# Attention output with tokens on partitions: unscaled probabilities, heads scaled on the way out of the bank, norm in one operation

## The chip, the cores and the metric

The kernel runs on one core of a Trainium2 chip. The metric is the time of one execution on the device, in microseconds (us). Inputs, weights and output are float32 in the chip's memory.

## The reference

2304 tokens of 512 numbers pass through three layers. Only the first, and the norm at the start of the second, are touched by the change.

```python
def _attn_ref(q, k, v):                      # (4, 8, 576, 64) each
    scores = scale * np.matmul(q, k.transpose(0, 1, 3, 2))
    mask = (rel >= 0) & (rel < window)       # window = 64
    scores = np.where(mask, scores, -1000000000.0)
    scores = scores - np.max(scores, axis=-1, keepdims=True)
    attn = np.exp(scores)
    attn = attn / (np.sum(attn, axis=-1, keepdims=True) + 1e-09)
    return np.matmul(attn, v)

def _moe_ref(x, w_gate, w_val, w_out, rms_g):   # x: (2304, 512)
    rms = np.sqrt(np.mean(x * x, axis=-1, keepdims=True) + 1e-06)
    xn = x / rms * rms_g
    g = xn @ w_gate
    silu = g * (1.0 / (1.0 + np.exp(-g)))
    val = xn @ w_val
    return silu * val @ w_out
```

The third layer routes each token to one of eight experts (512 to 1024 to 512, with a ReLU), and scales what comes back.

## The kernel before

The tokens are cut into 18 tiles of 128. `attention_front` loads a tile's queries, keys and values, `attention_tile` computes its attention and its norm, and leaves `xn`, the normed tile with the 512 numbers on partitions (four pieces of 128) as a high and a low half. The second layer, called FFN here, runs over groups of tiles, `GROUPS = [[0, 1], [2], [3], [4], [5]]` with `SIZES = [2, 2, 4, 4, 4, 2]` tiles in each: `ffn_step` multiplies by a block of the gate and value weights (L976 to L978, three matmuls for the products of high and low halves), applies the activation (L988, L993, L1001) and multiplies by the output weights (L1018 to L1020). In the first group `conv` loads the weights and splits them into halves on ScalarE (ACT) and VectorE (DVE), and `save` writes them to memory for the later groups. The attention of later tiles runs between the FFN matmuls of earlier groups. The experts come last.

What a tile does, by line:

- `mmc` (L680, L688) makes the scores. One bank holds four heads: 128 partitions are the 128 queries, four stretches of 128 columns are the four heads' keys. A query looks back 64 tokens, so the upper 64 queries need the 64 keys before the tile and its first 64, the lower 64 the tile's own 128. The host puts the previous tile's last 64 keys in front of each tile's own, so keys come as 192 columns per head pair, 384 KB per tile. Four mask matmuls (L680) and 16 score matmuls (L688) run, each in one 64x64 quarter of TensorE (PE); `c` is the half of the queries and `j` the head of a pair. A float32 matmul shows as two records.
- For each bank: the maximum (L707), its scaling (L711 or L713), four exponentials with their sums (L717), the guard against zero (L724 or L726), the reciprocal (L729), and `nm`, which multiplies the probabilities by it (L462 on DVE or GpSimd, called POOL, or L734 on ACT). Then four transposes (L751) and a copy out of the bank.
- `pv` (L768): 16 matmuls with the values as weights, so that the output has a head pair's 128 numbers on partitions and tokens as columns.
- `sqr` squares that bank into `xf` (L780), `weigh` multiplies it by the norm's weight g into `x` (L462, or L785 on ACT), and `sums` adds the squares over partitions by matmuls with ones (L795): four per tile for tiles 0 to 3, and one for the others, after `add` (L462) has added the four pieces. `mean` (L812, L814) and `root` (L819, on POOL) follow, giving `y`.
- A transpose of `y`, spread over 128 columns (L828), brings the factor onto all partitions, and `norm` multiplies `x` by it (L462). `hi` (L452, L456) and `lo` (L459) make the halves.

The order of the work comes from a planner. `Plan.op` gets for each step its costs on the engines that may do it, the buffers that it reads and writes, and a due time; a table `SHIFT` with a number per due time moves it, and a dictionary `K` holds the planner's other constants. From these the planner makes one fixed order of instructions for each engine and for SyncE (SP), which issues the loads in order. Where its reckoning finds TensorE idle, it places fillers (L624): matmuls on a tile of ones into a bank of their own, read by nobody. `K["warm"]` is the planner's time from which that bank goes to other work.

```python
pl.op(
    {"t": 1.28}, mmc, r=[qt, kt, both_b, masks], w=col, hold=halves, prio=pr + 2 * sg, tiled=True
)
```

Here `t` is TensorE, 1.28 is the planner's reckoned cost, `r` and `w` are what is read and written, and `prio` is the due time.

## Time and profile before

| | us |
|---|---|
| runs | 800.52, 800.59, 801.9 (median 800.59) |
| the profiled execution | 798.19 |
| its span, first to last instruction | 796.5 |
| TensorE busy | 785.2 |
| VectorE busy | 425.5 |
| ScalarE busy | 357.2 |
| GpSimd busy | 63.7 |

Busy times are unions of the recorded instructions of an engine. In the trace a line of TensorE reads: line of the program, operation, output and inputs by their names, the part of the array (64\*64 is a quarter), the moving operand's partitions and columns, the type, and the number of records. An instruction's end is modelled and overlaps the next one's start, so the cost of a group of matmuls is read from its start to the next group's start.

### The profile page before, as it was taken

How to read it: one execution, taken by the hardware profiler on the slowest of the kernel's cores; microseconds unless marked ns; L12 is line 12 of the kernel's file. 1: busy time of each engine (PE TensorE's matmuls, PEld its weight loads, DVE VectorE, ACT ScalarE, POOL GpSimd, SP SyncE). 2: the span in 40 equal slices, each digit the busy share in tenths (PEclk: the TensorE clock that was granted, in tenths of full speed). 3: DMA queues.
4: the chain of work that ended last, by engine and by line, in shares of the span. 5: the costliest groups of instructions: out<-in, count | busy, mean ns of one | idle time of the engine just before them, and what ended most of it. 6: DMA issues, size and time to landing. Idle time of an engine off the chain costs nothing.

```text
span 796.5 us, 14986 instructions
## 1 busy us (share of the span) xinstructions
PE 785.2 (99%) x5760; PEld 678.7 (85%) x5760; DVE 425.5 (53%) x1054; ACT 357.2 (45%) x959; POOL 63.7 (8%) x114
## 2 busy tenths in 40 slices
PE   9999999999999999999999999999999999999995
PEld 8998999988888888888888888899989998999981
DVE  5999998866452335633324322258447646576400
ACT  5988887556141244424341211325345444365311
POOL 2200000012000002000002000020110011020010
PEclk9999999999999999999999999999999999999998
DMA  8888888975541026430024830365195663676320
GB/s 276 310 281 284 296 288 293 292 257 165 182 173 53 28 76 210 153 112 1 1 106 159 306 116 1 110 212 182 60 300 183 202 198 110 214 241 228 139 77 19
DMA packets 51518, 137.30 MB, mean 172 GB/s; under 512 B 6564, under 2 KB 6564, under 8 KB 51444
## 3 DMA queue, kind: packets, MB, share of 16 engines
q1 hardware_dynamic: 48436, 126.78, 47.4%
q0 software_dynamic: 3008, 9.54, 3.2%
q8 instruction: 46, 0.75, 0.4%
q14 instruction: 28, 0.23, 0.1%
HBM read 112.07 MB, written 24.23 MB: 171 GB/s over the span
## 4 chain that ended last, share of the span: by engine, by line
PE 86%; issue 6%; DMA 5%; ACT 1%; DVE 0%; SPq 0%; POOLq 0%; POOL 0%
PE bank L976 13%; PE bank L977 13%; PE bank L978 13%; PE bank L1018 7%; PE bank L1019 6%; PE bank L1020 6%; DMA out_dram<-osb,meta 5%; PE bank L1522 3%; PE bank L1524 2%; PE bank L1523 2%; PE bank L768 2%; PE bank L751 2%; PE bank L688 2%; PE bank L1680 1%; PE bank L1682 1%
## 5 line engine op out<-in xcount | busy, mean ns | idle before, releaser
L976 PE MATMUL bank<-xn,w 128*128 128x256 f32 (+1 forms) x576 | 198.7, 345 | 0.0
L978 PE MATMUL bank<-xn,w 128*128 128x256 f32 (+1 forms) x576 | 193.8, 337 | 0.0
L977 PE MATMUL bank<-xn,w 128*128 128x256 f32 (+1 forms) x576 | 193.8, 336 | 0.0
L976 PEld LDWEIGHTS bank<-xn,w 128*128 128x128 f32 x576 | 108.8, 189 | 14.4 <-issue 0.6
L978 PEld LDWEIGHTS bank<-xn,w 128*128 128x128 f32 x576 | 108.9, 189 | 11.6
L977 PEld LDWEIGHTS bank<-xn,w 128*128 128x128 f32 x576 | 109.0, 189 | 11.3
L993 DVE SCALAR_TENSOR_TENSOR u<-u,bank 128x256 f32<-128x256 f32 (+1 forms) x72 | 39.6, 552 | 91.0 <-ACT u L988 90.6
L1018 PE MATMUL bank<-wo,h 128*128 128x512 f32 x216 | 87.4, 405 | 0.0
L1019 PE MATMUL bank<-wo,h 128*128 128x512 f32 x216 | 84.5, 391 | 0.0
L1020 PE MATMUL bank<-wo,h 128*128 128x512 f32 x216 | 84.4, 391 | 0.0
L988 ACT ACTIVATE u<-bank 128x256 f32<-128x256 f32 (+1 forms) x72 | 35.2, 489 | 98.1 <-PE bank L978 94.4
L459 DVE TENSOR_TENSOR w<-raw,w 128x512 fp32r<-128x512 f32 x112 | 72.8, 687 | 11.3 <-ACT w L452 10.7
L1001 DVE TENSOR_TENSOR u<-u,bank 128x256 f32<-128x256 f32 (+1 forms) x72 | 39.8, 553 | 70.8 <-PE bank L978 69.9
L452 ACT CAST h<-u 128x512 fp32r<-128x512 f32 (+1 forms) x67 | 34.8, 519 | 94.0 <-DVE u L1001 93.5
L452 ACT CAST w<-raw 128x512 fp32r<-128x512 f32 x90 | 51.3, 622 | 25.1 <-DMA raw<-in_moe_w_dram 13.0
L1522 PE MATMUL bank<-xT,w 128*128 128x240 f32 (+4 forms) x192 | 58.3, 304 | 0.0
L1524 PE MATMUL bank<-xT,w 128*128 128x240 f32 (+4 forms) x192 | 57.8, 301 | 0.0
L1523 PE MATMUL bank<-xT,w 128*128 128x240 f32 (+4 forms) x192 | 57.8, 301 | 0.0
L459 DVE TENSOR_TENSOR h<-u,h 128x256 fp32r<-128x256 f32 (+1 forms) x72 | 40.0, 556 | 23.7 <-ACT h L452 23.3
L717 ACT ACTIVATE s<-bank,m 128x128 f32<-128x128 f32 x144 | 50.8, 382 | 0.4
L1020 PEld LDWEIGHTS bank<-wo,h 128*128 128x128 f32 x216 | 40.6, 188 | 8.9
L1018 PEld LDWEIGHTS bank<-wo,h 128*128 128x128 f32 x216 | 40.7, 188 | 8.2 <-issue 0.9
(242 smaller groups left out, 1342.5 us busy)
## 6 DMA issues: line engine op xcount, KB each, us to landing
w<-whd SPq DMA_DIRECT2D x64, 512.0 KB, 4.3
raw<-in_moe_w_dram SPq DMA_DIRECT2D x64, 512.0 KB, 4.8
whd<-w SPq DMA_DIRECT2D x24, 512.0 KB, 6.1
val<-in_v_dram SPq DMA_DIRECT2D x18, 512.0 KB, 6.1
kt<-in_k_dram SPq DMA_DIRECT2D x18, 384.0 KB, 4.7
raw<-in_moe_w_gate_dram SPq DMA_DIRECT2D x12, 512.0 KB, 5.3
raw<-in_moe_w_out_dram SPq DMA_DIRECT2D x12, 512.0 KB, 5.2
raw<-in_moe_w_val_dram SPq DMA_DIRECT2D x12, 512.0 KB, 5.5
```

What stands on the lines that cost most here:

```text
L452: nc.scalar.copy(o, i)
L459: ve[e].tensor_tensor(out=o, in0=i, in1=h, op=ALU.subtract)
L717: nc.scalar.activation(out=s.t[:, h], in_=score()[:, h], func=AF.Exp, bias=mb.t[:, h:h + 1], scale=scale, accum_out=mb.t[:, 4 + h:5 + h],)
L976: nc.tensor.matmul(o, lhsT=h_, rhs=xn.t[:, 0, kk], start=(kk == 0), stop=False)
L977: nc.tensor.matmul(o, lhsT=h_, rhs=xn.t[:, 1, kk], start=False, stop=False)
L978: nc.tensor.matmul(o, lhsT=l_, rhs=xn.t[:, 0, kk], start=False, stop=(kk == KD - 1))
L1018: nc.tensor.matmul(o, lhsT=h.t[:, 0, c], rhs=wo.t[:, 0, f], start=(n == 0), stop=False)
L1019: nc.tensor.matmul(o, lhsT=h.t[:, 0, c], rhs=wo.t[:, 1, f], start=False, stop=False)
L1020: nc.tensor.matmul(o, lhsT=h.t[:, 1, c], rhs=wo.t[:, 0, f], start=False, stop=(n == NF - 1))
L1522: nc.tensor.matmul(o, lhsT=wh, rhs=x.t[:, 0, kk, 0:N], start=(kk == 0), stop=False)
L1523: nc.tensor.matmul(o, lhsT=wh, rhs=x.t[:, 1, kk, 0:N], start=False, stop=False)
L1524: nc.tensor.matmul(o, lhsT=wl, rhs=x.t[:, 0, kk, 0:N], start=False, stop=(kk == KD - 1))
```

## The change

Parts that are computed otherwise:

- Keys are loaded as 128 columns (256 KB). The scores of the upper 64 queries against the 64 keys before the tile read the previous tile's key buffer, so a tile has 24 score matmuls, 16 of 64 columns and 8 of 128 (L697 of the changed program). There are four key buffers where there were three.
- The probabilities go unscaled to the transposes; `nm` is gone. There is one guard and one reciprocal of eight columns per tile.
- `pv` (L828 of the changed program) has the probabilities as weights and the values as moving operand: the output has tokens on partitions and all eight heads' numbers as 512 columns.
- `xr` multiplies each head by its reciprocal while it copies the bank to `x`. `sqr` squares `x` on ACT and adds up along the row. `mean` and `root` stay; `norm` is one operation on DVE, x times the factor of its token times g. For that g is loaded on every partition (256 KB instead of 2 KB). `weigh`, `add`, `sums`, and the transpose of `y` are gone.
- `turn` (L871 of the changed program) transposes the four pieces of `x` into a bank, and `hi` and `lo` read that bank.
- A branch for scores that are made turned is there, for tiles below `K["st"]`, which is 0.

The planner's constants and its whole table are others. The diff, with the table cut to a line of each:

```diff
-    w_r=4, sl=1.2, n_q=4, n_kt=3, n_s=4, n_m=4, n_p=4, n_x=4, n_y=3, n_xf=1, n_val=3, pf=0.1, cold=6.0, late=1, f0=24.0, pw=110.0, pb=0.6, c1a=0, c1v=0, spe=4, lact=0, warm=86.204, wf=2.122, flead=24.233, nwv=1, port=1.0, t0=46.214, pp=93.267,
-    lead=1.781, clead=9.978, stag=2.552, stage=1.001, slack=-0.037, nt=2, look=-0.056, marg=0.752, dw=1.398, ewl=3.278,
-    ews=8.339, xld=43.407, xtn=7.222, mlead=14.712, vb=0.027, vb2=0.339, tb=-0.042, share=0.003, pls=9, phs=9, sf=0, hfs=1.431, stk=-0.015, rlead=7.936, span=0.317, wl=1.841,
+    w_r=4, sl=1.2, n_q=4, n_kt=4, n_s=4, n_m=4, n_p=4, n_x=4, n_xf=1, n_val=3, pf=0.1, cold=6.0, late=1, f0=24.0, pw=110.0, pb=0.6, c1a=0, c1v=0, st=0, lact=0, warm=40.111, wf=1.857, flead=24.233, nwv=1, port=1.0, t0=46.214, pp=93.267,
+    lead=1.781, clead=9.978, stag=2.552, stage=1.001, slack=0.069, nt=2, look=-0.005, marg=0.006, dw=1.434, ewl=3.278,
+    ews=8.339, xld=43.407, xtn=7.222, mlead=14.712, vb=0.304, vb2=0.465, tb=263.445, share=-0.155, pls=9, phs=9, sf=0, hfs=1.431, stk=-4.54, rlead=7.936, span=0.317, wl=1.841,
...
-    -38.8, -23.1, 59.5, 48.6, 13.7, 47.4, -3.4, -27.9, 3.4, -42.8, -38.2, -38.2, -88, -88.6, -42.9, -17.7, 12.7, -45.4, -59.5, -37.3, -7.7, 14.3, 20.9, -27.3,
...
+    14, 3.2, -22.1, -4.4, 3.7, -63.2, 9.9, -2.1, -52.9, -84.3, -89.9, -29.1, -41.5, -40.9, -31, -77.8, -38.7, -21.5, -22.6, -69.6, -71.3, -42.7, -0.5, -0.2,
...
-    g_sb = fixed("g_sb", [P, KD])
+    g_sb = fixed("g_sb", [P, DM])
...
-        {"s": 0.06}, lambda e: nc.sync.dma_start(out=g_sb.t, in_=rms_g.rearrange("(k p) -> p k", p=P)),
-        w=[g_sb], dma=0.22, prio=8,
+        {"s": 0.06}, lambda e: nc.sync.dma_start(out=g_sb.t, in_=rms_g.rearrange("(o d) -> o d", o=1).to_broadcast([P, DM])),
+        w=[g_sb], dma=0.95, prio=8,
...
-    tag("kt", "a", K["n_kt"], [P, 4, 192])
+    tag("kt", "a", K["n_kt"], [P, 4, P])
...
-    tag("m", "a", K["n_m"], [P, 8])
+    tag("m", "a", K["n_m"], [P, 18])
...
-    tag("y", "a", K["n_y"], [P, 2])
...
+    keys = {}
...
+        keys[t] = kt
...
-        pl.op({"s": 0.1}, load_t(k, kt, t), w=[kt], dma=1.4, prio=pr - K["wl"] + 0.1)
+        pl.op({"s": 0.1}, load_t(k, kt, t), w=[kt], dma=0.95, prio=pr - K["wl"] + 0.1)
...
+        turned_too = t < K["st"]
...
+        mb = Buf("m")
+        before = keys[max(t - 1, 0)]
+        parts = ((0, 0, 64, before, 64), (1, 0, P, kt, 0), (0, 64, 64, kt, 0))
...
             for i in range(4):
-                for c in range(2):
+                for c, o, n, src, at in parts:
                     for j, bk in enumerate(col):
                         nc.tensor.matmul(
-                            bk.t[half(c), i * P:(i + 1) * P], lhsT=qt.t[half(j), i, half(c)],
-                            rhs=kt.t[half(j), i, 64 * c:64 * c + P], start=False, stop=(i == 3),
+                            bk.t[half(c), i * P + o:i * P + o + n], lhsT=qt.t[half(j), i, half(c)],
+                            rhs=src.t[half(j), i, at:at + n], start=False, stop=(i == 3 and (c == 1 or o > 0)),
                         )
...
-            {"t": 1.28}, mmc, r=[qt, kt, both_b, masks], w=col, hold=halves, prio=pr + 2 * sg, tiled=True
+            {"t": 1.28}, mmc, r=[qt, kt, before, both_b, masks], w=col, hold=halves, prio=pr + 2 * sg, tiled=True
...
-            def guard(e, mb=mb):
-                if e == "a":
-                    nc.scalar.activation(out=mb.t[:, 4:8], in_=mb.t[:, 4:8], func=AF.Copy, bias=1e-9)
-                else:
-                    ve[e].tensor_scalar(out=mb.t[:, 4:8], in0=mb.t[:, 4:8], scalar1=1e-9, scalar2=None, op0=ALU.add)
-
-            def rc(e, mb=mb):
-                nc.vector.reciprocal(out=mb.t[:, 4:8], in_=mb.t[:, 4:8])
-
-            def nm(e, s=s, mb=mb):
-                if e == "a":
-                    for h in range(4):
-                        nc.scalar.activation(out=s.t[:, h], in_=s.t[:, h], func=AF.Copy, scale=mb.t[:, 4 + h:5 + h])
-                else:
-                    times(e, s.t, s.t, mb.t[:, 4:8].unsqueeze(2).to_broadcast([P, 4, P]))
-
-            pl.op({"v": 0.61}, mx, r=[sc], w=[mb], prio=ps_)
-            pl.op({"v": 0.08, "a": 0.11}, mxs, r=[mb], w=[mb], prio=ps_)
-            pl.op({"a": 1.48}, ex, r=[sc, mb], w=[s, mb], prio=ps_)
-            pl.op({"v": 0.08, "a": 0.11}, guard, r=[mb], w=[mb], prio=ps_)
-            pl.op({"v": 0.09}, rc, r=[mb], w=[mb], prio=ps_)
-            pl.op({"p": 1.02, "v": 0.61, "a": 1.18}, nm, r=[s, mb], w=[s], prio=ps_, lock="pv")
...
+            pl.op({"v": 0.19, "a": 0.1}, mxs, r=[(mb, hf)], w=[(mb, hf)], prio=ps_, lock="pv")
+            pl.op({"a": 1.48}, ex, r=[sc, (mb, hf)], w=[s, (mb, 2 + hf)], prio=ps_)
...
+        px_ = pr + 5 * sg
...
+        def rc(e):
+            nc.vector.reciprocal(out=mb.t[:, 8:16], in_=mb.t[:, 8:16])
+        pl.op(
+            {"v": 0.19, "a": 0.1}, guard, r=[sm] if turned_too else [(mb, 2), (mb, 3)], w=[(mb, 2), (mb, 3)], prio=px_ - 0.05,
+            lock="pv",
+        )
+        pl.op({"v": 0.19}, rc, r=[(mb, 2), (mb, 3)], w=[(mb, 2), (mb, 3)], prio=px_ - 0.04)
...
         def pv(e, bk=bk):
             for i in range(4):
-                for c in range(2):
-                    for j in range(2):
+                for j in range(2):
+                    for c in range(2):
                         hd = 2 * i + j
                         nc.tensor.matmul(
-                            bk.t[half(j), i * P + 64 * c:i * P + 64 * c + 64], lhsT=al.t[:, c, hd * D:(hd + 1) * D],
-                            rhs=pb_[j].t[:, i, half(c)], start=True, stop=True,
+                            bk.t[half(c), hd * D:(hd + 1) * D], lhsT=pb_[j].t[:, i, half(c)],
+                            rhs=al.t[:, c, hd * D:(hd + 1) * D], start=True, stop=True,
                         )
...
+        def xr(e):
+            r = mb.t[:, 8:16].rearrange("p (j i) -> p i j", j=2).unsqueeze(3).to_broadcast([P, 4, 2, D])
+            times(e, x.t.rearrange("p i (j d) -> p i j d", j=2), bk.t.rearrange("p (i j d) -> p i j d", i=4, j=2), r)
+
...
         def sqr(e):
-            nc.scalar.activation(out=sq.t, in_=pair(), func=AF.Square)
-
-        def weigh(e):
+            nc.scalar.activation(out=sq.t, in_=x.t, func=AF.Square, accum_out=mb.t[:, 16:17])
+
...
+                nc.scalar.activation(out=ms, in_=ms, func=AF.Copy, scale=1.0 / DM, bias=1e-6)
             else:
-                times(e, x.t, pair(), g_sb.t.unsqueeze(2).to_broadcast([P, KD, P]))
-
-        pl.op({"t": 1.1}, pv, r=[al, *pb_], w=[bk], hold=[x, sq], prio=px_, rows=0.5)
...
-        def sums(e, bk=bk):
-            for kk in range(n):
-                nc.tensor.matmul(
-                    bk.t[:, 0:2], lhsT=sq.t[:, kk], rhs=ones.t, start=(kk == 0), stop=(kk == n - 1)
-                )
...
-        n = KD
-        if t >= K["spe"]:
-            n = 1
-            pl.op({"p": 1.25, "v": 0.67}, add, r=[sq], w=[sq], prio=pn_, lock="pv")
-        pl.op({"t": 0.224 * n}, sums, r=[sq, ones], w=[bk], hold=[y], prio=pn_, rows=0.05)
...
+            nc.gpsimd.tensor_tensor(out=mb.t[:, 17:18], in0=mb.t[:, 16:17], in1=mhalf.t, op=ALU.pow)
+
+        def norm(e):
+            nc.vector.scalar_tensor_tensor(
+                out=x.t, in0=x.t, scalar=mb.t[:, 17:18], in1=g_sb.t.rearrange("p (k t) -> p k t", t=P), op0=ALU.mult, op1=ALU.mult
+            )
+
+        pl.op({"t": 1.1}, pv, r=[al, *pb_], w=[bk], hold=[x], prio=px_, rows=0.5)
+        pl.op({"v": 0.66}, xr, r=[bk, (mb, 2), (mb, 3)], w=[x], prio=px_ + 0.05)
+        pl.op({"a": 0.66}, sqr, r=[x], w=[sq, (mb, 4)], prio=px_ + 0.06)
+        pl.op({"a": 0.1, "v": 0.19}, mean, r=[(mb, 4)], w=[(mb, 4)], prio=pn_)
+        pl.op({"p": 0.72}, root, r=[(mb, 4), mhalf], w=[(mb, 5)], prio=pn_, lock="pv")
+        pl.op({"v": 0.65}, norm, r=[x, (mb, 5), g_sb], w=[x], prio=pn_)
...
-            {"t": 0.11}, lambda e: nc.tensor.transpose(bk2.t[:, 0:P], y.t[:, 1:2].to_broadcast([P, P]), ident.t),
-            r=[y, ident], w=[bk2], prio=pn_, rows=0.5,
-        )
-
-        def norm(e):
-            both("v", x.t, x.t, bk2.t[:, 0:P].unsqueeze(1).to_broadcast([P, KD, P]), ALU.mult)
-
-        pl.op({"v": 0.65}, norm, r=[x, bk2], w=[x], prio=pn_)
...
+        def turn(e):
+            for kk in range(KD):
+                nc.tensor.transpose(bk2.t[:, kk * P:(kk + 1) * P], x.t[:, kk], ident.t)
+
+        def pair():
+            return bk2.t.rearrange("p (k t) -> p k t", t=P)
+
+        pl.op({"t": 0.43}, turn, r=[x, ident], w=[bk2], prio=pn_ + 0.02, rows=0.5)
         xn_w[p_].append(pl.op(
-            cost(512, "hs"), lambda e: hi_i(e, xn.t[:, 0, :, js], x.t), r=[x], w=[(xn, (j, 0))], prio=pn_, lock="pv"
+            cost(512, "hp"), lambda e: hi_i(e, xn.t[:, 0, :, js], pair()), r=[bk2], w=[(xn, (j, 0))], prio=pn_ + 0.02
         ))
         xn_w[p_].append(pl.op(
-            cost(512, "ls"), lambda e: lo_i(e, xn.t[:, 1, :, js], x.t, xn.t[:, 0, :, js]),
-            r=[x, (xn, (j, 0))], w=[(xn, (j, 1))], prio=pn_, lock="pv",
+            cost(512, "lp"), lambda e: lo_i(e, xn.t[:, 1, :, js], pair(), xn.t[:, 0, :, js]),
+            r=[bk2, (xn, (j, 0))], w=[(xn, (j, 1))], prio=pn_ + 0.02,
         ))
         attn_ops.append(xn_w[p_][-1])
...
-        if name == "q":
+        if name in ("q", "k"):
             a = turned(a)
-        elif name == "k":
-            a = turned(a)
-            own = a.reshape(a.shape[0], P, HEADS // 2, P)
-            a = np.concatenate([np.roll(own[..., WINDOW:], 1, axis=0), own], axis=3).reshape(a.shape[0], P, -1)
```

The order of the loads at the start (SP). `q`, `kt` and `val` are a tile's queries, keys and values; the shapes are partitions by float32 numbers. Before, and then in the changed program:

```order
L656 DMA q_178<-in_q_dram 128x512
L656 DMA q_202<-in_q_dram 128x512
L656 DMA kt_229<-in_k_dram 128x768
L656 DMA val_266<-in_v_dram 128x1024
L656 DMA kt_285<-in_k_dram 128x768
L656 DMA val_317<-in_v_dram 128x1024
```

```order
L658 DMA kt_179<-in_k_dram 128x512
L658 DMA q_200<-in_q_dram 128x512
L658 DMA val_222<-in_v_dram 128x1024
L658 DMA q_269<-in_q_dram 128x512
L658 DMA kt_311<-in_k_dram 128x512
L658 DMA kt_313<-in_k_dram 128x512
```

The keys of the second tile are the fifth load in both; the first two tiles' queries and keys are smaller, and the first tile's values now stand before the second tile's queries.

TensorE just before the first FFN matmul (L976 before, L1017 in the changed program). `s` are probabilities, `p` their transposes, `xf` the squares, `xn` the normed tile:

```order
L688 MATMUL bank_800<-kt_702,q_612 64x128
L795 MATMUL bank_830<-ones,xf_767 128x2 x4
L751 MATMUL bank_844<-ident,s_581 128x128 x4
L976 MATMUL bank_852<-xn,w_604 128x256
L977 MATMUL bank_852<-xn,w_604 128x256
```

```order
L697 MATMUL bank_764<-kt_667,q_684 64x64
L697 MATMUL bank_765<-kt_667,q_684 64x64
L828 MATMUL bank_805<-val_529,p_713 64x64 x2
L828 MATMUL bank_805<-val_529,p_755 64x64 x2
...
L871 MATMUL bank_831<-ident,x_647 128x128 x4
L1017 MATMUL bank_837<-xn,w_635 128x256
```

Where the sums and a transpose of another tile's probabilities stood, a value product and the turn of a tile's `x` stand. Over the whole program the fillers go from 280 to 198: before the first FFN matmul 200 become 152 (46 and 26 before the first and the second score block become 34 and 22), after it 80 become 46. DVE has 1007 instructions for 1082, ACT 795 for 838, POOL 131 for 137.

## Rows read from the trace of the kernel before

**Rows 1.** The page: busy us of each engine; TensorE's granted clock.

```profile
PE 785.2 (99%) x5760; PEld 678.7 (85%) x5760; DVE 425.5 (53%) x1054; ACT 357.2 (45%) x959; POOL 63.7 (8%) x114
...
PEclk9999999999999999999999999999999999999998
```

**Rows 2.** Waits of TensorE: who, for whom, us in total, times, longest.

```profile
PE warm L624 <- DVE ones_b L535: 1.4, 1, 1.4
PE bank L688 <- DMA kt<-in_k_dram: 0.4, 1, 0.4
```

**Rows 3.** Stages: us; busy of PE, PEld, DVE, ACT, POOL; clock; DMA share; GB/s.

```profile
0.00:33.00 33.00, 31.11 (x545) 28.21 (x546) 22.87 (x63) 24.41 (x96) 8.78 (x39) 1.00 0.83 280
33.00:58.00 25.00, 25.00 (x305) 23.26 (x304) 22.72 (x54) 21.45 (x71) 1.28 (x2) 1.00 0.88 297
58.00:150.00 92.00, 91.98 (x822) 84.01 (x822) 85.93 (x195) 74.32 (x186) 3.88 (x5) 1.00 0.88 294
```

**Rows 4.** Fillers alone, by stage: TensorE busy (records); clock; DMA share; GB/s.

```profile
0.00:33.00 33.00, 14.07 (x200) 1.00 0.83 280
33.00:58.00 25.00, 5.30 (x74) 1.00 0.88 297
58.00:100.00 42.00, 0.84 (x6) 1.00 0.85 291
```

**Rows 5.** TensorE's timeline, start of the program: start, us, instruction, records, [idle before].

```profile
1.40 4.14 PE L624 MATMUL warm<-ones_b 128*128 128x128 bf16 x46 [1.40 <-DVE ones_b L535]
...
9.19 1.10 PE L688 MATMUL bank<-kt,q 64*64 64x128 f32 x32 [0.40 <-DMA kt<-in_k_dram]
```

**Rows 6.** TensorE's timeline, 26 us to the first FFN matmul.

```profile
26.37 1.06 PE L624 MATMUL warm<-ones_b 128*128 128x128 bf16 x16
27.26 0.28 PE L828 MATMUL bank<-ident,y 128*128 128x128 f32 x1
27.46 1.15 PE L768 MATMUL bank<-p,val 128*64 128x64 f32 x32
28.55 0.65 PE L751 MATMUL bank<-ident,s 128*128 128x128 f32 x4
...
29.37 1.04 PE L688 MATMUL bank<-kt,q 64*64 64x128 f32 x32
30.35 1.05 PE L795 MATMUL bank<-ones,xf 128*128 128x2 f32 x8
31.26 0.64 PE L751 MATMUL bank<-ident,s 128*128 128x128 f32 x4
31.65 0.36 PE L976 MATMUL bank<-xn,w 128*128 128x256 f32 x1
```

**Rows 7.** TensorE's timeline in the steady stage, 96 to 104 us.

```profile
96.48 0.60 PE L751 MATMUL bank<-ident,s 128*128 128x128 f32 x4
96.91 0.27 PE L828 MATMUL bank<-ident,y 128*128 128x128 f32 x1
96.94 0.36 PE L976 MATMUL bank<-xn,w 128*128 128x256 f32 x1
97.14 0.28 PE L977 MATMUL bank<-xn,w 128*128 128x256 f32 x1
...
102.66 0.28 PE L795 MATMUL bank<-ones,xf 128*128 128x2 f32 x2
102.80 0.48 PE L1018 MATMUL bank<-wo,h 128*128 128x512 f32 x1
103.12 0.39 PE L1019 MATMUL bank<-wo,h 128*128 128x512 f32 x1
```

**Rows 8.** By line and form: count, busy us, mean ns, idle before.

```profile
L462 DVE TENSOR_TENSOR s<-s,m 128x512 f32<-128x512 f32 x27 | 18.6, 689 | 0.5
...
L462 DVE TENSOR_TENSOR x<-bank,g_sb 128x512 f32<-128x512 f32 x13 | 9.0, 691 | 11.3 <-ACT xf L780 10.4 <-PE bank L768 0.8
...
L795 PE MATMUL bank<-ones,xf 128*128 128x2 f32 x60 | 8.0, 230 | 0.0
```

More of the change, by code (lines that the diff above doesn't have):

```diff
@@ L716, in ex @@
+            def ex(e, s=s, score=score, hf=hf):
                 for h in range(4):
+                    at = 4 * hf + h
                     nc.scalar.activation(
[L718 to L726 removed]
@@ L757, in attention_tile, with guard @@
             )
+        px_ = pr + 5 * sg
+        def guard(e):
+            o = mb.t[:, 8:16]
+            i = sm.t[:, 0:32].rearrange("p (h z) -> p h z", z=4)[:, :, 0] if turned_too else o
+            if e == "a":
+                nc.scalar.activation(out=o, in_=i, func=AF.Copy, bias=1e-9)
+            else:
+                nc.vector.tensor_scalar(out=o, in0=i, scalar1=1e-9, scalar2=None, op0=ALU.add)
+        def rc(e):
+            nc.vector.reciprocal(out=mb.t[:, 8:16], in_=mb.t[:, 8:16])
@@ L782, in weigh, with mean @@
[L782 removed]
+            nc.scalar.activation(out=sq.t, in_=x.t, func=AF.Square, accum_out=mb.t[:, 16:17])
+        def mean(e):
+            ms = mb.t[:, 16:17]
             if e == "a":
[L784 to L789 removed]
```

93 lines of the change are left out of this document (58 added, 35 removed), and 79 rows, old and new, of the table SHIFT.

## The prediction

> **What bounds the kernel now.** I read the page first, for the engine that sets the end. TensorE (PE) is busy 99% of the span, VectorE (DVE) 53% and ScalarE (ACT) 45%, and the granted clock stands at 9 tenths or more in all but the last slice, so on its upper level of 2.4 GHz [rows 1]. Next the waits of TensorE: there are two, 1.4 us for the ones that its first matmul reads and 0.4 us for a block of keys [rows 2]. Every other pause is filled by something. The busy time by stages shows it: between 58 and 150 us TensorE works 91.98 of 92.00 us [rows 3]. Last, how much of that is filler, matmuls on a tile of ones whose result nobody reads: 200 records before 33 us, 74 up to 58 us, 6 after it [rows 4]. Back to back, such records stand 56 ns apart (26.37 to 27.26 us for 16, [rows 6]), so the 280 of them hold at least 15.7 us.
>
> It follows that an operation taken off DVE, ACT or GpSimd (POOL) is worth nothing by itself. The time moves by three things alone: what TensorE has to compute, how many fillers stand in its program, and a wait that appears. So the sum is made in TensorE's time, from start to start of neighbouring rows, since the ends overlap.
>
> **The change, part by part.**
>
> *Norm: sums and the turn of y out, the turn of x in.* Four tiles summed the squares with eight records: 30.35 to 31.26 us, 0.91 us each [rows 6]. The other 14 did it with two: 102.66 to 102.80, plus the 0.09 us by which the next matmul (0.48) outlasts its sister (0.39), so 0.23 us [rows 7]; 4 x 8 + 14 x 2 are the 60 records of the group [rows 8]. Out: 4 x 0.91 + 14 x 0.23 = 6.9 us. The transpose of y took 0.03 us to the next start and lengthened that matmul by 0.08 (0.36 against 0.28), 0.11 us [rows 7]; out: 18 x 0.11 = 2.0 us. In: four 128x128 transposes of x per tile, the same form as those of the scores, which took 96.48 to 96.91, 0.43 us [rows 7]; 18 x 0.43 = 7.7 us. **Together -1.2 us.** Were the short groups as dear to enter as the ones at 30 us and the turn free of that, it would be -2; the other way round, 0. That is small against what follows.
>
> *Score block.* The host no longer puts the previous window's keys in front of each tile's own, so the first 64 columns read the tile before. 16 matmuls of 128 columns (32 records) become 24: 16 of 64 and 8 of 128, 48 records. Each of the four quadrants gets the same columns as before. No row shows a 64x64 tile with 64 columns. Bounds: if only columns count, nothing; if every record costs what one does now, half again: 29.37 to 30.35 is 0.98 us for 32 [rows 6], so +0.49 x 18 = 8.8 us. (Below nothing it can't be: no column goes.) The nearest row is the product with the values: 32 records of 64 columns, two at a time, 27.46 to 28.55, 1.09 us [rows 6]. The columns that follow one another are as many (16 x 64 in two lanes, 16 x 128 in four), and it takes 0.11 us more. I take that: 18 x 0.12 = **+2.2 us**.
>
> *The product with the values* swaps weights and moving operand: 16 matmuls, 128 rows, 64 columns, both ways. Nothing.
>
> *Fillers.* The change has 198 where there were 280 records: 152 instead of 200 before the first FFN matmul, 46 instead of 80 behind it. At 56 ns that is 48 x 0.056 = 2.7 us and 34 x 0.056 = 1.9 us. A filler taken out gains only if the work behind it is ready. The first piece can be traced: before the first score block stand 34 fillers instead of 46, before the second 22 instead of 26, so the second comes 16 x 0.056 = 0.9 us sooner. It waited for its keys, until 9.19 us [rows 5], behind q, q, keys, values, keys, 1,792 KB. Now keys, q, values, q, keys come first, 1,536 KB; at the 280 GB/s of this stage [rows 3] the 0.26 MB less are 0.9 us. The two agree. Up to the first FFN matmul (31.65 us, [rows 6]) I take the gain in full, because DVE and ACT lose work ahead of it: normalising the probabilities (0.69 us each half, on DVE 27 of 36) and the weighing by g (0.69 us) go, and the scaling on leaving the bank (bounded by the 0.69 us of the weighing, which reads a bank too) and one norm stay [rows 8]. From scores to the value product each half loses 0.69 us of its chain; from there to xn the scaling and the turn (0.69 + 0.43) replace the sums and the turn of y (0.91 + 0.11). Behind the first FFN matmul DVE and ACT are 22.72 and 21.45 us of 25.00 busy [rows 3]; the fillers there cover waits for converted weights, which this change leaves alone. I count half: 1.0 us. **Together -3.65 us**; the ends are 0 (all comes back as waits) and -5.5 (all 4.6 gained, and the two pauses of the start shrink by 0.9).
>
> *What costs nothing.* 18 x 128 KB of keys less, against 0.25 MB for g, which is now loaded on every partition: the DMA engines are 83 to 88% busy up to 150 us [rows 3], yet no matmul but one waits for them. The scaling, the squares with their running sum, the one guard and one reciprocal per tile: DVE and ACT sit beside a full TensorE. If that cover went, the scaling would cost its 0.69 us per tile. The high and low halves of xn now read a bank and not x, and keep it longer; eight banks bound this, and TensorE would show it as a wait. The expert part and the end keep their work.
>
> *Sum.* -1.2 + 2.2 - 3.65 = -2.65 us on the profiled execution: 798.19 - 2.65 = 795.5. The median of the runs is 800.59, 2.4 above it: **797.9 us**. About 0.2% (1.6 us) is what a measurement of this kernel can tell from no change.
>
> **The rivals.**
>
> *The gain is deeper.* Score block by columns alone, fillers to their end: -1.2 + 0 - 5.5 = -6.7, 793.9 us. For it: the four quadrants get equal columns, and a later piece of one can run while the next is served. Against: the waits for converted weights.
>
> *The fillers were covering real waits.* Then 82 fillers less turn into 4.6 us of idle TensorE, and -1.2 + 2.2 = +1.0: 801.6 us, no change that can be told. For it: ACT and DVE are 86 to 91% busy from 33 to 58 us [rows 3]. Against: the start, where the keys do come sooner.
>
> *Slower: the pieces of the score block cost by the record.* 8.8 instead of 2.2: -1.2 + 8.8 - 3.65 = +3.95, 804.5 us. It decides against the change from 0.98 + (1.2 + 3.65)/18 = 1.25 us per block. For it: 32 records in 0.98 us are 31 ns each, and nothing in the trace shows them closer. Against: those records are 128 columns wide and share four quadrants, so the width alone explains the 31 ns. The Trainium skill, "TensorE: Matmul & The Clock Gate", section "Wait — 56ns, not 53.3ns?", says that matmuls never start closer than about 25 ns however narrow they are. By that rule the block would be an estimated 48 x 25 ns = 1.2 us and the total 799.7 us, within a measurement of no change; no row here has pieces narrow enough to show it.
>
> *The clock falls.* The granted clock is 1.00 in every stage up to 150 us, fillers in between [rows 3, 4]. If, with 34 fillers fewer, a quarter of the 20 us of real work between 33 and 58 us ran at 1.2 GHz, it would take 5 us more: 797.9 + 5 = 802.9. Against: TensorE has no wait there [rows 2], and 46 fillers remain. The same page of the Trainium skill, section "Part 4: PE-mode transpose", says that transposes don't count as busy time for the clock. That speaks against putting 72 of them where sums stood; the rows show transposes between other matmuls at full clock, and none alone.
>
> *Less than it says.* The new branch that takes the scores already turned (for tiles below a constant that is 0) runs for no tile; without it the sum stands.
>
> **How the numbers follow.** The forecast 0.42, deeper 0.17, covered waits 0.22, score pieces 0.15, clock 0.04. The range goes from the deeper gain to the score pieces, 793.9 to 804.5, and leaves out about half of either and little else, some 0.16. The forecast's own range is 795.5 to 800.5 (q and the fillers by half their bounds). Faster than 799.0: three quarters of the forecast and the deeper gain, 0.48. Slower than 802.2: score pieces, clock and a quarter of the covered waits, 0.25. The rest, 0.27, is no change.
>
> **What would show it.** Right: score blocks of 1.05 to 1.15 us, 198 fillers, the second score block near 8.3 us, the first FFN matmul near 29, TensorE without a new wait, granted clock 1.00. Wrong: score blocks over 1.25 us; a first FFN matmul at 31 us or later with waits for DVE or ACT before it; a new wait of TensorE for x or for a bank beyond 58 us, which would mean that the longer way from values to xn, not the fillers, decides.

## The result, and the profile after

The changed kernel takes 791.96 us (median of five runs, 791.65 to 792.63), the kernel before 801.07 us in the same comparison (five runs, 800.52 to 801.9). The ratio is 0.9887, 95% interval 0.9874 to 0.9901: faster by 1.1%, some 9 us. I had said 797.9 us and a range from 793.9, so the time lies below the range. The profiled execution took 792.13 us with a span of 790.4.

The page, for [rows 1]:

```profile
PE 779.6 (99%) x5960; PEld 677.7 (86%) x5960; DVE 402.1 (51%) x979; ACT 342.1 (43%) x934; POOL 58.7 (7%) x108
...
PEclk9999999999999999999999999999999999999998
```

TensorE's waits, for [rows 2]:

```profile
PE warm L626 <- DVE ones_b L538: 1.1, 1, 1.1
PE bank L1059 <- ACT h L455: 0.4, 1, 0.4
PE bank L794 <- DVE x L465: 0.2, 1, 0.2
```

The stages, for [rows 3], columns as there:

```profile
0.00:33.00 33.00, 31.86 (x634) 29.80 (x635) 23.86 (x60) 26.34 (x107) 5.76 (x37) 1.00 0.85 300
33.00:58.00 25.00, 25.00 (x327) 22.85 (x324) 21.23 (x47) 23.26 (x83) 0.61 (x1) 1.00 0.83 292
58.00:150.00 92.00, 91.76 (x856) 85.56 (x855) 80.53 (x181) 69.54 (x175) 4.11 (x4) 1.00 0.88 295
```

The fillers alone by the same stages, for [rows 4] (TensorE busy, records, clock, DMA share, GB/s):

```profile
0.00:33.00 33.00, 13.69 (x178) 1.00 0.85 300
33.00:58.00 25.00, 1.45 (x24) 1.00 0.83 292
58.00:100.00 42.00, 0.00 (x0) 1.00 0.82 277
```

TensorE's timeline from the start to the first FFN matmul, for [rows 5, 6]:

```profile
1.14 3.81 PE L626 MATMUL warm<-ones_b 128*128 128x128 bf16 x34 [1.14 <-DVE ones_b L538]
...
5.31 1.89 PE L697 MATMUL bank<-kt,q 64*64 64x64 f32 x48
7.13 1.40 PE L626 MATMUL warm<-ones_b 128*128 128x128 bf16 x22
...
8.70 1.09 PE L697 MATMUL bank<-kt,q 64*64 64x64 f32 x48
...
26.02 1.09 PE L697 MATMUL bank<-kt,q 64*64 64x64 f32 x48
27.04 1.15 PE L828 MATMUL bank<-val,p 128*64 128x64 f32 x32
28.12 0.66 PE L871 MATMUL bank<-ident,x 128*128 128x128 f32 x4
28.54 0.36 PE L1017 MATMUL bank<-xn,w 128*128 128x256 f32 x1
```

By line and form, the new operations on VectorE and TensorE (count, busy us, mean ns, idle before):

```profile
L854 DVE SCALAR_TENSOR_TENSOR x<-x,m,g_sb 128x512 f32<-128x512 f32 x18 | 13.4, 746 | 3.5 <-POOL m L851 1.9 <-POOL nop L1222 1.7
...
L465 DVE TENSOR_TENSOR x<-bank,m 128x512 f32<-128x512 f32 x18 | 12.4, 687 | 6.9 <-PE bank L828 6.6
...
L871 PE MATMUL bank<-ident,x 128*128 128x128 f32 x72 | 10.8, 274 | 0.0
```

TensorE is as full as before, and no wait of note has come. The trace's first clock row, with 1.00, begins at 7.04 us (before: 4.38); ahead of it fillers start 107 ns apart, behind it 56. The fillers are 198, most of them up to 33 us and none after 58 us (a record across a border counts in both stages). The second score block starts at 8.70 us where it started at 9.19, the first FFN matmul at 28.54 where it stood at 31.65. Of the loads ahead of that block only the keys are smaller; the queries are 128x512 as before. The scaling takes 687 ns on VectorE and the norm 746 ns. A score block lasts 26.02 to 27.04, 1.02 us; the first one, ahead of the clock's rise, took 1.82 (5.31 to 7.13).

Here are the times from each of TensorE's records to the start of its next one, added up by group over the two traces:

| group | before, us (records) | after | difference |
|---|---|---|---|
| fillers | 17.65 (280) | 13.39 (198) | -4.3 |
| score matmuls and masks | 17.34 (576) + 4.89 (72) | 19.05 (864) + 4.46 (72) | +1.3 |
| sums, and turn of y | 5.59 (60) + 1.45 (18) | 0 | -7.0 |
| turn of x | 0 | 7.46 (72) | +7.5 |
| FFN matmuls | 459.5 (2376) | 456.6 (2376) | -2.8 |
| all others | 278.8 (2377) | 278.7 (2377) | 0 |
| before the first matmul, from the start of the last | 1.4 + 9.9 | 1.1 + 9.6 | -0.6 |
| span | 796.5 | 790.4 | -6.1 |

The FFN matmuls are the same in number and shape. They are cheaper because other work breaks into their row less often: the first one behind another kind of work lasts about 0.09 us longer from start to start (as 0.36 against 0.28 in [rows 7]), and there are 58 such entries for 85. Of the 85, 23 stood behind the sums and the turn of y, and 6 behind fillers; of the 58, 9 stand behind the turn of x, and 1 behind a filler. The score matmuls alone cost 1.7 us more, 0.8 of it in the first block; the masks are 0.4 us cheaper, as the 0.4 us of waiting for keys behind them [rows 2] is gone.

From about 555 us on, where the last FFN matmul stands (557.8 before, 552.8 after), the difference stays at 5 to 6 us to the end: the expert part gave nothing.

### The profile page after: what moved, and what is told of

Same layout as the page of the kernel before. It is cut to its first block, busy times and chain, and to the rows that moved or that the text cites. A ratio compares the mean times of both kernels' runs of the same rounds, so it can differ in the third digit from the quotient of the medians.

```text
span 790.4 us, 15251 instructions
## 1 busy us (share of the span) xinstructions
PE 779.6 (99%) x5960; PEld 677.7 (86%) x5960; DVE 402.1 (51%) x979; ACT 342.1 (43%) x934; POOL 58.7 (7%) x108
## 4 chain that ended last, share of the span: by engine, by line
PE 88%; issue 5%; DMA 5%; DVE 1%; ACT 0%; POOLq 0%; POOL 0%
PE bank L1017 13%; PE bank L1019 13%; PE bank L1018 13%; PE bank L1059 6%; PE bank L1060 6%; PE bank L1061 6%; DMA out_dram<-osb,meta 4%; PE bank L1563 3%; PE bank L1565 3%; PE bank L1564 3%; PE bank L828 2%; PE bank L697 2%; PE bank L794 2%; PE warm L626 2%; PE bank L1723 2%
## 5 line engine op out<-in xcount | busy, mean ns | idle before, releaser
L1017 PE MATMUL bank<-xn,w 128*128 128x256 f32 (+1 forms) x576 | 197.4, 343 | 0.0
L1017 PEld LDWEIGHTS bank<-xn,w 128*128 128x128 f32 x576 | 108.9, 189 | 13.5 <-issue 0.6
L1034 DVE SCALAR_TENSOR_TENSOR u<-u,bank 128x512 f32<-128x512 f32 (+1 forms) x72 | 39.7, 552 | 110.6 <-ACT u L1029 110.3
L1029 ACT ACTIVATE u<-bank 128x512 f32<-128x512 f32 (+1 forms) x72 | 35.4, 492 | 116.9 <-PE bank L1019 116.2
L1042 DVE TENSOR_TENSOR u<-u,bank 128x512 f32<-128x512 f32 (+1 forms) x72 | 39.8, 552 | 84.4 <-PE bank L1019 83.1
L455 ACT CAST h<-u 128x512 fp32r<-128x512 f32 (+1 forms) x63 | 32.6, 517 | 109.7 <-DVE u L1042 107.1
L455 ACT CAST w<-raw 128x512 fp32r<-128x512 f32 x86 | 49.7, 619 | 23.4 <-DMA raw<-in_moe_w_dram 11.2
L462 DVE TENSOR_TENSOR h<-u,h 128x512 fp32r<-128x512 f32 (+1 forms) x72 | 39.9, 555 | 22.9 <-ACT h L455 22.0
```

What stands on the lines that cost most here:

```text
L455: nc.scalar.copy(o, i)
L462: ve[e].tensor_tensor(out=o, in0=i, in1=h, op=ALU.subtract)
L1017: nc.tensor.matmul(o, lhsT=h_, rhs=xn.t[:, 0, kk], start=(kk == 0), stop=False)
```

## The experiments

Each was compared with the kernel before on the same chip and at the same time. That kernel's own level moved by up to 2 us between comparisons, so a time is best read beside the kernel before of its own comparison.

**The kernel before, profiled again.** No edit.

> The kernel before, profiled again. Theory A (the first profiled execution, 798.19 us, was one of the shortest this program has, and the others stand at 800.5 to 801.9): this profile shows a span of 798.8 to 800, 2 to 3 us above 796.5, and its extra time can be found in a stage. Theory B (the profiler's execution is always shorter than a plain one for this program): the profile shows 796.5 again beside plain runs of 800.5 to 802.

Measured: 801.72 us (12 runs), the kernel before beside it 801.35 (23 runs, 800.56 to 802.75); profiled 801.57, span 799.9. Theory A holds. TensorE's waits in this execution:

```profile
PE bank L751 <- ACT s L717: 0.8, 1, 0.8
PE bank L688 <- DMA kt<-in_k_dram: 0.4, 2, 0.2
PE bank L751 <- DVE m L726: 0.4, 1, 0.4
PE bank L1522 <- DVE eh L1533: 0.3, 1, 0.3
PE bank L1680 <- DVE eh L1533: 0.2, 1, 0.2
```

and VectorE's timeline near 315 us:

```profile
314.63 1.28 DVE L707 TENSOR_REDUCE m<-bank 128x4 f32<-128x512 f32 x2
318.23 0.69 DVE L707 TENSOR_REDUCE m<-bank 128x4 f32<-128x512 f32 x1 [2.32 <-remote]
```

Between the second and the third maximum VectorE stood still for 2.3 us in which, in the first trace, the three ran as one. The block of scores before it had taken 1.40 us where such a block takes 0.97; the trace names no wait for that. Behind it TensorE waits 0.8 and 0.4 us for probabilities (L751). Behind the transposes it is 2.4 us later than the first trace, 0.3 of them from the start, and 3.7 at its end: the rest comes in three steps of 0.3 to 0.4 us at 546, 647 and 732 us, with waits for VectorE in the expert part (L1522 and L1680). The profile on which I built the forecast was of an execution that had none of this.

Four later profiles in this order, of other comparisons, don't have the wait near 315 us either (pieces in 16 blocks, normalisation twice, no guard, copy twice), and the kernel before stood at 799.2 to 799.4 us beside them. The run with fewer fillers, taken beside this one, does have it:

```profile
316.32 0.69 DVE L712 TENSOR_REDUCE m<-bank 128x4 f32<-128x512 f32 x1 [2.35 <-remote]
```

**Score block in pieces, in the kernel before.**

```diff
-                for c in range(2):
+                for c, o, n in ((0, 0, 64), (1, 0, P), (0, 64, 64)):
...
-                            bk.t[half(c), i * P:(i + 1) * P], lhsT=qt.t[half(j), i, half(c)],
-                            rhs=kt.t[half(j), i, 64 * c:64 * c + P], start=False, stop=(i == 3),
+                            bk.t[half(c), i * P + o:i * P + o + n], lhsT=qt.t[half(j), i, half(c)],
+                            rhs=kt.t[half(j), i, 64 * c + o:64 * c + o + n], start=False, stop=(i == 3 and (c == 1 or o > 0)),
```

> The kernel before with its score block in 24 matmuls instead of 16, from the same 192 columns of keys, all orders kept. If the pieces cost as I took them, +2.2 us (0.12 us per block); if by the record, +8.8 us; if by columns alone, 0. The changed kernel's own timeline (1.03 us per block from start to start, against 0.98) says +1.

Measured: 810.51 us against 801.35, ratio 1.0108 (1.0094 to 1.0123), +9.2 us. By the size that would be the rival "by the record", but the blocks say otherwise: ten of the 18 take 1.02 or 1.03 us from start to start, 0.05 more than before, and the neighbouring pairs 0.88 and 1.07 (0.87 and 0.97 before). Two take 3.18 and 4.73. TensorE's timeline at the first of them (start, us, records, idle before):

```profile
30.55 1.09 PE L688 MATMUL bank<-kt,q 64*64 64x64 f32 x47
33.53 0.27 PE L688 MATMUL bank<-kt,q 64*64 64x64 f32 x1 [1.90 <-issue]
...
36.48 0.41 PE L977 MATMUL bank<-xn,w 128*128 128x256 f32 x1
36.69 0.41 PE L978 MATMUL bank<-xn,w 128*128 128x256 f32 x1
```

and at the second, the later of two neighbouring blocks:

```profile
320.44 0.78 PE L688 MATMUL bank<-kt,q 64*64 64x128 f32 x25
321.64 0.33 PE L688 MATMUL bank<-kt,q 64*64 64x64 f32 x3 [0.41 <-issue]
322.32 0.45 PE L688 MATMUL bank<-kt,q 64*64 64x128 f32 x6 [0.35 <-issue]
323.06 0.30 PE L688 MATMUL bank<-kt,q 64*64 64x64 f32 x2 [0.29 <-issue]
...
325.17 0.79 PE L1018 MATMUL bank<-wo,h 128*128 128x512 f32 x1
```

The first stops 1.9 us before its last record, the second comes in bursts with pauses of 0.3 to 0.4 us, and "issue" means that the profile shows nothing that was waited for. Behind each the clock is at half (stages of 2 us, and of 4 us for the last line):

```profile
32.00:34.00 2.00, 0.47 (x3) 0.40 (x3) 1.79 (x5) 0.62 (x2) 0.00 (x0) 0.96 0.15 55
...
36.00:38.00 2.00, 2.00 (x12) 2.00 (x11) 0.00 (x0) 1.58 (x3) 0.41 (x1) 0.50 1.03 378
...
324.00:328.00 4.00, 3.58 (x19) 2.64 (x17) 2.34 (x7) 2.07 (x14) 0.00 (x0) 0.50 0.85 284
```

From 32 to 34 us TensorE is busy 0.47 us of 2; from 36 to 38 the granted clock is 0.50, and matmuls that start 0.12 us apart at full clock start 0.21 apart. The trace's rows at 0.50 go from 33.9 to 40.7 and from 324.0 to 330.8 us, so they cost up to 3.4 us each, an estimate from half their length. All four runs show it, with mean granted clocks of 0.988 to 0.992 (0.996 or 0.997 in the kernel before). So the price was two stoppages and the clock after them, not the width of the pieces.

**Pieces in 16 of the 18 blocks.** Whole blocks at those two places.

```diff
-                for c, o, n in ((0, 0, 64), (1, 0, P), (0, 64, 64)):
+                for c, o, n in ((0, 0, P), (1, 0, P)) if blk in (4, 15) else ((0, 0, 64), (1, 0, P), (0, 64, 64)):
```

> The kernel before with pieces in 16 of its 18 score blocks, whole blocks at the two places (the fifth block and the second of the pair near 315 us) where the run with pieces in all blocks showed pauses inside the block and half the clock behind them. If the pieces themselves cost 0.05 us per block (the timeline of that run), and the +9 us came from those two places: +0.5 to +1.5 us over the kernel before and granted clock 0.996. If pieces cost everywhere in a way that the starts don't show, or the pauses move to other blocks: +5 us or more.

Measured: 800.54 us (12 runs) against 799.35 (23 runs), ratio 1.0014 (1.0004 to 1.0025): +1.2 us, as expected of 16 x 0.05 = 0.8. The pieces are cheap, and whether a block of them stops depends on its place in the program. What makes it stop these runs don't show.

**Fewer fillers in the kernel before.** Of its 140 pairs of fillers 41 are left out.

```diff
+        z = calls[0]
+        calls[0] += 1
+        if 17 <= z < 23 or z in (34, 35) or (36 <= z < 100 and z % 4 == 0) or (z >= 100 and (z * 17) // 40 != ((z + 1) * 17) // 40):
+            return
```

> The kernel before with 198 fillers, taken out at the places where the change has fewer, all else in its order. Theory 'fillers are time': -4 to -4.6 us. Theory 'fillers cover waits that only the rest of the change removes': 0 to -1.5 us and new waits of TensorE for converted weights or for x before 58 us, of 2 us or more in sum.

Measured: 800.58 us, and widely spread (798.21 to 806.09, 12 runs), ratio 0.9999 (0.9979 to 1.0019). TensorE's waits:

```profile
PE bank L693 <- DMA kt<-in_k_dram: 0.8, 1, 0.8
PE bank L756 <- ACT s L722: 0.8, 1, 0.8
PE bank L756 <- DVE m L731: 0.7, 2, 0.4
PE bank L1457 <- DMA t2k<-xs: 0.6, 1, 0.6
```

Beside the second profile of the kernel before, of the same comparison, this trace tells the fillers apart. At the first FFN matmul it is 0.3 us ahead with 48 fillers (2.7 us) less: most had come back, 0.8 us as a wait for keys ahead of the second block; and the first score block takes 1.55 us (5.70 to 7.25) where it took 1.04, as the clock row of 1.00 begins at 6.81 us in this execution and at 4.72 in the other. By 100 us it is 1.8 us ahead, a further 1.5 for the 34 fillers (1.9 us) that are missing there, and it ends 1.6 us ahead. The runs, though, spread so widely that no gain can be told; in those of 806.09 and 805.54 us the mean granted clock was 0.991 and 0.992. In the old order, then, as far as this one trace shows, the early fillers did cover waits, the late ones hardly.

**Fillers back into the changed kernel.** 41 pairs doubled, to 280 records.

```diff
+        more = 11 <= z < 17 or z in (26, 27) or (28 <= z < 76 and z % 3 == 0) or (z >= 76 and (z * 17) // 23 != ((z + 1) * 17) // 23)
-        for _ in range(2):
+        for _ in range(4 if more else 2):
```

> The changed kernel with 82 more fillers at about the places where the kernel before had them, all else in its order: 280. If fillers are time, +4 to +4.6 us, near 796.3. If half of the gain of fewer fillers had been given back as waits (as I counted behind the first FFN matmul), +3.6.

Measured: 797.43 us (797.11 to 798.13, 9 runs), against 791.70 for the next run on the same chip: +5.7 us, more than the 4.6 of the fillers themselves. Put into this order, they are time in full.

**The changed kernel again.** No edit.

> The changed kernel, profiled again. If its first profile is like its other runs, 790 to 791 us of span and no wait of TensorE above 0.5 us after the start, near 315 us included. If the missing wait was a matter of that execution, a wait of about 1 us there and 2 us more.

Measured: 791.70 us (791.11 to 793.39) against 799.17 for the kernel before (14 runs, 798.19 to 801.24), ratio 0.9903 (0.9888 to 0.9918). Its trace has no wait above 0.4 us behind the start. So the change is worth 7.5 us here and 9.1 us in the first comparison; it is mostly the kernel before that moves.

**The changed kernel without its late fillers.** The 46 behind the first FFN matmul are left out.

> The changed kernel without its 46 fillers behind the first FFN matmul. If they are time, -2.6 us, near 789.4, which would beat it. If they cover waits, 0, and TensorE waits 2 to 3 us between 30 and 45 us; if the clock falls in the pauses, up to +3 us and granted clocks under 0.996 in some runs, as with fewer fillers in the kernel before (0.991 and 0.992 in its runs of 806.09 and 805.54 us).

Measured: 792.04 us (791.00 to 792.54), no gain. TensorE's waits:

```profile
PE bank L876 <- DVE x L859: 1.2, 1, 1.2
...
PE bank L1498 <- DMA t2k<-xs: 1.0, 1, 1.0
```

Beside the changed kernel's second profile it is 1.3 us ahead at 527 us, so half of the fillers' 2.6 us was time there; near 575 us it waits 1.0 us for the rows that were scattered for the experts (L1498). At the end nothing is left of the lead.

**The split keys taken back out.** The changed kernel with 192 columns of keys and 16 matmuls per block, and with three buffers of keys and of queries.

```diff
-    tag("kt", "a", K["n_kt"], [P, 4, P])
+    tag("kt", "a", K["n_kt"], [P, 4, 192])
...
-                for c, o, n, src, at in parts:
+                for c in range(2):
```

> The changed kernel with whole score blocks: keys of 192 columns again (384 KB per tile, prepared by the host), 16 matmuls per block, three key and three query buffers for want of room, TensorE's, VectorE's and ScalarE's orders as in the change. By the sum: 0.9 to 2.2 us less TensorE time, and 0.9 us later keys at the start, so 790.5 to 792.5 us. If the split keys were the gain (less to load), 794 us or more.

Measured: 795.47 us (792.83 to 795.8, 5 runs), 3.5 over the changed kernel in the first comparison, and so beyond what I expected of the sum. Two of the five runs, 792.83 and 793.39 us, are less than 1.5 over it, and the ratio to the kernel before beside it, which stood at 801.35, is 0.9911 (0.9897 to 0.9926): the loss is a matter of three runs, the profiled one among them. TensorE's timeline at the second block in that one:

```profile
5.90 1.40 PE L626 MATMUL warm<-ones_b 128*128 128x128 bf16 x22
...
9.73 1.10 PE L697 MATMUL bank<-kt,q 64*64 64x128 f32 x32 [2.09 <-DMA kt<-in_k_dram]
```

and the stages behind it:

```profile
8.00:10.00 2.00, 0.27 (x9) 0.30 (x13) 0.00 (x0) 1.87 (x12) 0.00 (x0) 1.00 1.06 424
...
12.00:14.00 2.00, 2.00 (x20) 2.00 (x19) 0.55 (x5) 1.82 (x9) 0.00 (x0) 0.50 1.06 401
```

The wait for keys grew to 2.09 us, TensorE was busy 0.27 us of the two before 10 us, and from 12 to 14 us the clock was 0.50 (the trace's row goes from 10.9 to 14.3). The Trainium skill, "TensorE: Matmul & The Clock Gate", section "What's actually happening", says that the lower clock is the default and activity lifts it; this trace agrees, with 0.50 behind the wait.

**The same with 16 more fillers ahead of the first two blocks.**

```diff
-        for _ in range(2):
+        for _ in range(4 if z < 6 or z in (17, 18) else 2):
```

> The changed kernel with whole score blocks and 384 KB of keys, as in the earlier run, and 16 more fillers ahead of its first two blocks, as many as the kernel before has more. If that run's loss was the 2.1 us of idle TensorE at the start and the half clock behind it (10 to 14 us): TensorE bridges the wait, the second block still starts near 9.7 us, and the time falls from 795.5 to about 793.5. If the loss was the later keys alone: no change from 795.5.

Measured: 792.30 us (791.96 to 792.81, 5 runs), ratio to the kernel before 0.9909 (0.9895 to 0.9922). TensorE bridges the wait and starts the block at about the same time:

```profile
7.79 1.63 PE L629 MATMUL warm<-ones_b 128*128 128x128 bf16 x26
...
9.58 1.04 PE L700 MATMUL bank<-kt,q 64*64 64x128 f32 x32
```

The ratio to the kernel before is that of the earlier run, which had no such fillers, since the kernel before moved between the two; the trace, with its wait and its stretch at half clock gone, shows what the fillers do. So the split keys, with all their loads saved, are worth nothing that these runs can tell: what they save at the start they spend in 18 x 0.05 = 0.9 us of pieces. The gain comes from the rest of the change: the other computing, the order, and the planner's constants.

**The normalisation twice, in the kernel before.**

```diff
+                    if e == "v":
+                        times(e, s.t, s.t, ones.t[:, 0:1].unsqueeze(2).to_broadcast([P, 4, P]))
                     times(e, s.t, s.t, mb.t[:, 4:8].unsqueeze(2).to_broadcast([P, 4, P]))
```

> The kernel before, every normalisation of probabilities that runs on VectorE done twice (first times one, then times the reciprocal), orders kept: 27 x 0.69 = 18.6 us more on VectorE, and 0.69 us more from the scores to the transposes of each half. Theory 'VectorE lies beside a full TensorE' (the prediction's): 0 to +1 us. Theory 'the chain from the scores to the transposes sets the time in some stages, above all near 315 to 323 us, where the second profile of the kernel before shows TensorE waiting 1.2 us for it': +3 to +6 us, with waits of TensorE for the probabilities there and before 58 us.

Measured: 804.47 us against 799.17, ratio 1.0060 (1.0047 to 1.0073), +5.3 us. TensorE's waits, after the two at the start, are at the transposes of probabilities (here L753):

```profile
PE bank L753 <- DVE m L726: 1.6, 2, 0.9
...
PE bank L753 <- DVE lg L456: 0.6, 1, 0.6
PE bank L753 <- DVE s L462: 0.3, 1, 0.3
```

Against the first trace it falls behind by 0.3 to 1.1 us each at such transposes at 40, 57, 81, 93, 186 and 321 us. VectorE, busy 53%, is not free where this chain runs.

**The copy of the probabilities twice, in either kernel.**

```diff
-                cost(512, "hp"), lambda e, bk=bk, pb=pb: hi_i(e, pb.t, bk.t.rearrange("p (i t) -> p i t", t=P)),
+                cost(512, "hp"), lambda e, bk=bk, pb=pb: [hi_i(e, pb.t, bk.t.rearrange("p (i t) -> p i t", t=P)) for _ in range(2)],
```

> The kernel before with the copy of the transposed probabilities out of the bank done twice (33 on ScalarE, 3 on VectorE), orders kept: about 0.55 us more in the chain of each half. If the chain has no slack, +3 to +6 us as with the normalisation twice; if ScalarE lies beside a full TensorE, 0 to +1.

> The changed kernel with the same copy done twice (30 on ScalarE, 6 on VectorE), orders kept. If the change, by taking the normalisation (0.69 us a half) out of that chain, gave it slack: less than half of what the kernel before loses by it. If its order uses up the slack: as much.

Measured: 804.75 us against 799.18 before, +5.6; and 797.07 us against 791.70 and 791.96 for the changed kernel, +5.1 to +5.4. The changed kernel loses as much. Its waits, at the value product (L828):

```profile
PE bank L828 <- ACT p L455: 2.1, 4, 0.6
...
PE bank L828 <- DVE p L459: 0.5, 1, 0.5
```

So the change did not leave slack in this chain, as if its order had used it up.

**Without the guard, in the kernel before.**

```diff
             def guard(e, mb=mb):
+                pass
```

> The kernel before without the guard (the 1e-9 added to each sum of exponentials, 36 small operations of 0.16 us on VectorE or 0.2 us on ScalarE), all else and the orders kept. It leaves out that addition. Theory 'the chain from scores to transposes sets the time in several places': -0.5 to -2 us, since each half's chain is 0.2 to 0.3 us shorter. Theory 'it has slack': 0.

Measured: 799.42 us (11 runs) against 799.18, ratio 1.0002 (0.9992 to 1.0012). A chain that is 0.2 to 0.3 us shorter per half, in an order made for the longer one, gains nothing that these runs can tell.

**Both kernels without their tables.**

```diff
 SHIFT = [
...
```

> The kernel before without its table (all due times as computed; three buffers of queries and of transposed probabilities for want of room). Tells with the next run how much of the difference is the order. If the change's gain is mainly the work on TensorE and the shorter chains, the distance to the next run is like that of the tuned pair, 6 to 12 us; if mainly the table, it is under 4 us.

> The changed kernel without its table (all due times as computed), 198 fillers. Expected slower than the changed kernel by 10 us or more, as the table was fitted to it; the distance to the kernel before without its table is the point.

Measured: 811.29 and 799.89 us, both against 799.35 for the kernel before (ratios 1.0143, 1.0126 to 1.0159, and 1.0003, 0.9993 to 1.0012). The distance is 11.4 us. The planner put 354 fillers (22.75 us of TensorE from start to start) into the one and 198 (13.39 us) into the other. So the gain doesn't come out of the fitted table alone; without both tables the distance is larger. But the planner's other constants still differ in this pair, and the kernel before has three buffers there where it had four. One constant bears on the fillers directly: `K["warm"]` is 86.204 in the kernel before and 40.111 in the changed one. The last filler stands at 81.3 and 84.0 us in the two programs with the first value, and at 34.5 and 35.3 in the two with the second. Of the 354 fillers 128 start after 40 us, of the 280 it is 54, and of either 198 none.

## Why the prediction was wrong

*What bounds the kernel.* The reading of TensorE as full, with fillers in it, held. The conclusion "an operation taken off VectorE is worth nothing by itself" agrees with the run without the guard (0), but an operation put onto VectorE cost 5.3 us: it does not lie free beside TensorE. The fillers stand where the planner sees nothing ready. That the shorter work on VectorE and ScalarE is what lets a new plan do with fewer of them is my reading, and it is argued, not shown: the planner's constants, `warm` above all, were changed together with it. I had the 82 fillers counted, and that was right.

*Fillers:* forecast -3.65, measured -4.3 in the traces, and 5.7 when put back. Halving the later 34 was the error, small; even in the old order most of their time was gained, while of the 48 that I took in full most came back there. Of the signs three came: 198 fillers (counted beforehand), first FFN matmul at 28.54 (forecast "near 29"), second block at 8.70 ("near 8.3"). The score blocks of 1.05 to 1.15 us did not: they took 1.02.

*Norm:* forecast -1.2. The sums and the turn of y went out and the turn of x came in, which is +0.4 by itself. Their entries into the FFN matmuls fell from 23 to 9, and 14 x 0.09 = 1.3 us, so the term measures about -0.8 and was nearly right. The FFN matmuls got 2.8 us cheaper in all. The other 13 of the 27 entries saved, 1.2 us, stood behind fillers (5) and behind other short groups (8); for them, as for any gain from the new order of such groups, the sum had no term.

*Score block:* forecast +2.2 (18 x 0.12; the 0.11 read from the rows gives 2.0). Measured are 0.05 us per block in the steady part, 0.9 in all; the other 0.8 of the +1.7 in the score matmuls is the first block of this one execution, which ran ahead of the clock's rise and took 1.02 in the changed kernel's second profile. The nearest row (0.11 more for the value product) was too dear, and the columns alone were the better rule. The estimate of 1.2 us per block by the 25 ns of the Trainium skill, "TensorE: Matmul & The Clock Gate", section "Wait — 56ns, not 53.3ns?", is too long for matmuls in four quarters of the array: the 48 records of a block take 1.02 us, 21 ns each.

*The rest:* 0.6 us at the two ends, of which the sum had nothing. The sum on the profiled execution was forecast as -2.65 and came out as 792.13 - 798.19 = -6.06. The rival "the gain is deeper" came near it with -6.7, by luck: it had the fillers at -5.5 and the score block at 0, and nothing for the entries.

*The step that failed most:* "The median of the runs is 800.59, 2.4 above it". I added these 2.4 us to the forecast and to every rival, as if they were a cost outside the trace that any kernel bears. In the one execution that was compared with it they were waits inside the program, 2.1 us near 315 us and 1.3 later, that the first profile lacked (the kernel before, profiled again). In later comparisons the same program stood only 1.0 to 1.2 us above that first profile. The changed kernel has hardly any such distance: its profile is 792.13, its median 791.96. Without the 2.4 us my forecast would have been 795.5; nearly all of the 3.5 us that were still missing are the sum's own, -6.06 for -2.65.

*The other rivals.* "The fillers were covering real waits" is true of the early fillers in the kernel before (2.4 of 2.7 us came back by the first FFN matmul, part of it by the later clock of that execution) and hardly of the late ones; the changed kernel gained by having 82 fewer, and got nothing by losing its last 46 too. "Slower by the record" did not come, though the pieces alone in the old order cost 9.2 us, through stoppages that I had not thought of. Once up, the clock did not fall: 1.00 in each stage to 150 us, with the 72 transposes and without 82 fillers.

*Open.* A rival that no run tests: the kernel before planned anew with the changed kernel's constants, `warm` = 40.111 above all, might lose its late fillers too, and in its old order leaving out 34 of them gained 1.5 us in the trace. So how much of the gain needs the other computing isn't settled. Which of the two pieces, the normalisation out of the chain of probabilities or the norm without sums over partitions, lets the planner do without fillers was not tried apart either: each alone would need its own order. Why VectorE stands still for 2.3 us near 315 us in some executions of the kernel before, and why a block of pieces stops, is not settled.

## What to carry to other kernels

Before a distance between one profiled execution and the median is added to a forecast, profile the kernel twice: the distance may be a wait that only some executions have. Where a planner fills idle time with dummy work, find out which of it covers waits: taken out of the old order the early fillers gave 0.3 of 2.7 us and the late ones 1.5 of 1.9, put into the new one they cost more than their time. A chain a little shorter paid nothing in an order that stayed (no guard). When a planner's constants change together with the computing, run the old computing with the new constants too. An edit that is nearly free in one order (pieces, 0.05 us a block) can cost 9 us in another, so measure parts of a change in the order in which they will run.

## What the hardware did that I had not expected

- Streams of short matmuls stopped without a releaser: 1.9 us once, and five pauses of 0.3 to 0.4 us in one block, in the kernel before with pieces. The changed kernel, in its two profiles, runs such blocks in 0.88 to 1.07 us but for one each at the start: 1.82 us ahead of the clock's rise, and 1.64 with a wait for keys.
- A pause of 1.9 us on TensorE was followed by 6.8 us at granted clock 0.50, one of 2.1 us in another run by 3.4 us; at half clock that costs up to half of the stretch, 3.4 and 1.7 us by this estimate.
- The clock rose at different times in executions of one kernel: its first row of 1.00 begins at 7.04 and 5.10 us in the two profiles of the changed kernel, and at 4.38 and 4.72 in those of the kernel before.
- The same program stands at 801.35 us (800.56 to 802.75, 23 runs) in one comparison and at 799.18 us (797.51 to 802.26, 21 runs) in another (799.35 in a third, on the same chip as the first), while the changed one lies between 791.1 and 793.4 in its ten.
